# A twice-split channel MLP: p1 of two block pairs per group made of smaller products, their sums finished in their own PSUM tiles, in a new order

## The chip, the cores and the metric

The kernel runs on one core of a Trainium2 chip. The time is device microseconds of one execution; before the change the median of three runs is 792.29 us (792.07 to 792.38). The profiled execution is a further one. The core's engines are TensorE (PE; PEld is its weight load), VectorE (DVE), ScalarE (ACT), GpSimd (POOL) and SyncE (SP), each with a queue of its own that is worked off in order. Here SP issues nearly all transfers and POOL the rest.

## The reference

Hash attention over 4 batches, 8 heads, 768 positions of 64 features, then an MLP mixer over tokens and channels. The part that matters here is the last line, the channel MLP:

```python
xt = x.transpose(0, 2, 1)
h = np.maximum(xt @ w_tok1, 0.0) @ w_tok2
u = x + h.transpose(0, 2, 1)
h2 = np.maximum(u @ w_ch1, 0.0) @ w_ch2      # u: (4, 768, 512), w_ch1: 512x1536, w_ch2: 1536x512
return (u + h2).astype(np.float32)
```

All of it is in float32. A check on the attention's inputs (the `look`s) runs beside the channel MLP; a careful branch behind it is not taken with these inputs.

## The kernel before

The kernel has three stages: `attention` to about 310 us, `tokens` to 387 us, and `channels` to the end. The change lies in `channels`.

`channels` works on 3072 columns (4 batches of 768) in three groups s = 0, 1, 2 of 1024, a group being two slices of 512. Each group has a first layer (`hidden`, or `hidden_first` and `hidden_pair`), whose results go into four tiles R[0] to R[3], and a second layer (`outputs`, with `whole_product` and six calls of `product`). A matrix product is split in two by two blocks and computed with seven block products instead of eight (p1 to p7): the operands of p2 to p7 are blocks or sums of blocks, and the results are sums of the seven. `weight_sums` and `inputs` make such sums of the weights and of the columns.

In the first group the first layer's seven products are computed as they are (`hidden`, six times). In the groups s = 1 and 2 the rows come in three block pairs (t = 0, 1, 2, each of two blocks of 128 rows): `hidden_first` does t = 0 and `hidden_pair` t = 1 and 2. There p2, p3, p4, p6 and p7 (and p5 in `hidden_pair`) are split once more: each is a `Smaller`, seven products of 128 rows by 256 columns. `one` issues the first of them, `rest` three more into the same PSUM pair and `three` the last three into the pair where they are added to something else. Between these, `keep` (ScalarE) copies the first product out, `unite` (ScalarE) copies the sum of the first two, and `add` (VectorE, two instructions) makes the smaller results out of these in SBUF. p1, not a `Smaller`, is four products of 128 rows by 512 columns per block pair (`opened`); half of it is issued in the pair before (`open_next`). PSUM is four bank pairs, b0 to b3, taken in the order of `ring`; a `bank_pair` waits until all that used the pair before it has ended.

The right operands of a `Smaller` are made by `right_sums` (four VectorE instructions of 256 columns); its left operands, sums of the weights' quarters, are made once, in the preparation: `prepare` gives a list of jobs that the first group's `hidden` works off, one in the middle and one at the end of each call. A `parts` job makes four sums on VectorE (lines 1202 to 1205) in a tile of its own name, `seen`, or in a second area, and SP stores them to DRAM (`hidden_passed`, `passed`) with the quarters themselves (lines 1213 to 1223). Later `fetch_hidden_left` (line 871), `fetch_fifth` (879) and `fetch_left` (1273) bring them back on SP, each when the place has been read. `seen` has one buffer: a job that takes it waits until the store out of it has landed. The `look`s load into the same tile through POOL (line 1506) and work on it with two ScalarE activations (lines 1488 and 1496).

The order on each engine is the order of the program (a manual schedule). Two blocks in SBUF, `area(0)` and `area(1)`, hold the fetched left operands in front (`left_at`) and behind them output blocks: `output_at(0)` to `output_at(2)` in the one and `output_at(3)` in the other. In `hidden_first` p2's first product is copied into `output_at(2)` (`e2`, line 932 of `keep`). In `outputs` the results of the second layer's products take these blocks too, and `store` adds them to the output through POOL (line 1403).

## Time and profile before

The profiled execution took 793.06 us, its span from the first to the last instruction 791.3 us. The granted TensorE clock is 0.999.

| stretch | from, us | to, us |
|---|---|---|
| first group, first layer (with the preparation) | 387.2 | 459.1 |
| first group, second layer | 459.1 | 523.8 |
| second group, first layer | 523.8 | 591.15 |
| second group, second layer | 591.15 | 655.85 |
| third group, first layer | 655.85 | 721.75 |
| third group, second layer | 721.75 | 791.3 |

A line of the timeline has the start in the span, the length, the engine, the line of the kernel, what is written from what, its shape and how often; in square brackets the engine's idle time before it and what ended it. A TensorE record counts half a float32 product here, so "x6" is three products. Tile names are the program's: `second` is `area(0)` and `area(1)`, `TA` and `TB` hold the column sums, `SW` and `WC` the first layer's weights, `b` a PSUM pair. SPq and POOLq are the issue queues.

### The profile page before, as it was taken

The numbers are of one execution on the slowest core, as the hardware profiler recorded it, in microseconds if no ns is written. First come the engines' busy times: TensorE is split into PE (matmuls) and PEld (weight loads), VectorE is DVE, ScalarE is ACT, GpSimd is POOL, SyncE is SP. The second block draws the span as 40 slices with busy tenths as digits, with TensorE's granted clock in tenths as the row PEclk, the third lists the DMA queues.
The fourth block names the chain that finished last, engine by engine and source line by source line (L and its number), as shares of the span: only waits on it lengthen the run. The fifth ranks groups of instructions, "written<-read, shape, count | busy, mean of one in ns | idle before, by whom it ended". The sixth has DMA issues, their size and how long they took to land.

```text
span 791.3 us, 12505 instructions
## 1 busy us (share of the span) xinstructions
PE 784.1 (99%) x4721; PEld 476.3 (60%) x4721; DVE 656.8 (83%) x886; ACT 472.9 (60%) x817; POOL 53.7 (7%) x77
## 2 busy tenths in 40 slices
PE   9999999999999999999999999999999999999997
PEld 5444444444444444455544458877787887776886
DVE  5989898988987677999697798869879787978984
ACT  6688888888888886333323233536676674674331
POOL 1000000000000000011121010110001121000001
PEclk9999999999999999999999999999999999999999
DMA  4435353538352424795686995797847688830556
GB/s 164 163 123 163 123 164 123 163 124 248 144 175 87 142 60 164 210 265 119 119 267 230 343 367 182 228 303 200 274 128 231 242 243 213 252 92 0 184 161 140
DMA packets 102016, 144.85 MB, mean 183 GB/s; under 512 B 30200, under 2 KB 71616, under 8 KB 101952
## 3 DMA queue, kind: packets, MB, share of 16 engines
q1 hardware_dynamic: 93936, 119.15, 45.8%
q0 software_dynamic: 7728, 24.64, 14.0%
q8 instruction: 38, 0.62, 0.3%
q10 hardware_dynamic: 288, 0.21, 0.1%
q14 instruction: 26, 0.21, 0.1%
HBM read 101.01 MB, written 35.52 MB: 173 GB/s over the span
## 4 chain that ended last, share of the span: by engine, by line
PE 88%; issue 6%; DVE 2%; DMA 2%; POOL 1%; SPq 0%; ACT 0%; POOLq 0%; DVEq 0%; ACTq 0%
PE b L783 39%; PE sc L356 20%; PE acc L410 16%; PE t L656 5%; PE t L696 5%; PE sums L434 2%; PE hp L301 1%; DMA out<-second 1%; DMA hidden_left<-WC 0%; PE idle L473 0%; POOL out L1403 0%; PE hw L325 0%; POOL seen L1506 0%; DVE R L832 0%; DVE second L993 0%
## 5 line engine op out<-in xcount | busy, mean ns | idle before, releaser
L363 ACT ACTIVATE e<-sc 128x768 f32<-128x768 f32 x192 | 154.5, 810 | 6.4 <-PE sc L356 6.1
L356 PE MATMUL sc<-qk 64*128 64x384 f32 x768 | 152.6, 483 | 0.0
L783 PE MATMUL b<-R,second 128*128 128x256 f32 (+1 forms) x522 | 131.5, 409 | 0.0
L410 PE MATMUL acc<-e,vn 128*32 128x384 f32 x1536 | 127.0, 486 | 0.0
L783 PEld LDWEIGHTS b<-R,second 128*128 128x128 f32 x522 | 99.4, 190 | 29.1 <-issue 17.2
L395 DVE TENSOR_TENSOR esd<-esd,e 128x768 f32<-128x768 f32 x96 | 92.0, 958 | 10.4 <-ACT e L363 0.5
L410 PEld LDWEIGHTS acc<-e,vn 128*32 128x32 f32 x1536 | 50.1, 110 | 73.8 <-issue 73.4
L356 PEld LDWEIGHTS sc<-qk 64*128 64x128 f32 x768 | 68.2, 188 | 41.7 <-issue 37.2
L789 ACT COPY c<-b 128x256 f32<-128x256 f32 (+1 forms) x96 | 40.3, 426 | 80.6 <-PE b L783 70.4
L783 PE MATMUL b<-XT,WC 128*128 128x256 f32 (+1 forms) x228 | 74.0, 470 | 0.0
L356 PE MATMUL sc<-bits 64*128 64x384 bf16 x384 | 62.8, 324 | 0.1
L783 PEld LDWEIGHTS b<-XT,WC 128*128 128x128 f32 x228 | 43.3, 190 | 25.4 <-issue 20.0
L391 DVE SCALAR_TENSOR_TENSOR esd<-e 128x768 f32<-128x768 f32 x32 | 30.6, 956 | 23.4 <-ACT e L363 23.4
L783 PE MATMUL b<-XT,SW 128*128 128x256 f32 (+1 forms) x156 | 43.8, 413 | 0.4 <-DVE c L971 0.3
L656 PE MATMUL t<-x,W 128*128 128x512 f32 x96 | 41.8, 594 | 0.0
L356 PEld LDWEIGHTS <-bits 64*128 64x128 bf16 x384 | 18.6, 94 | 33.4 <-issue 9.7
L416 ACT ACTIVATE num<-acc,vsum 128x384 f32<-128x384 f32 x32 | 18.6, 581 | 29.8 <-PE acc L410 29.4
L783 PEld LDWEIGHTS b<-XT,SW 128*128 128x128 f32 x156 | 29.5, 190 | 11.0 <-issue 5.1
L716 POOL DMA_DIRECT2D XT<-second x8 | 9.8, 1228 | 383.1 <-DVE second L715 360.9
L455 ACT COPY rec<-rec 32x384 f32<-32x384 f32 x64 | 32.7, 510 | 5.0 <-DVE rec L449 4.2
L783 PE MATMUL b<-TA,WC 128*128 128x256 f32 (+1 forms) x92 | 33.7, 476 | 0.9 <-ACT c L932 0.9
L398 DVE TENSOR_TENSOR esd<-esd,e 128x768 f32<-128x768 f32 x32 | 30.5, 954 | 1.9
(245 smaller groups left out, 1219.3 us busy)
## 6 DMA issues: line engine op xcount, KB each, us to landing
second<-left SPq DMA_DIRECT2D x20, 768.0 KB
raw<-in_moe_w_ch SPq DMA_DIRECT2D x16, 768.0 KB
qk<-in_qk SPq DMA_DIRECT2D x15, 768.0 KB
second<-left SPq DMA_DIRECT2D x18, 576.0 KB
seen<-in_qk POOLq DMA_DIRECT2D x21, 384.0 KB, 4.8
WC<-hidden_left SPq DMA_DIRECT2D x18, 448.0 KB
vn<-in_v SPq DMA_DIRECT2D x16, 384.0 KB
vt<-in_vT SPq DMA_DIRECT2D x16, 384.0 KB
```

The source lines that it names most:

```text
L356: nc.tensor.matmul(sc[:, i, :HALF], t[rows, 1, P * c : P * c + P], t[rows, 0, qs], start=start, stop=not start,)
L363: nc.scalar.activation(e, sc[:, :, :HALF], ACT.Exp, scale=SCALE)
L391: nc.vector.scalar_tensor_tensor(self.d, es[0], NR * EPS, es[1], op0=ALU.add, op1=ALU.add,)
L395: nc.vector.tensor_tensor(self.d, self.d, e, op=ALU.add)
L398: nc.vector.tensor_tensor(self.d, self.d, self.es[-1], op=ALU.add)
L410: nc.tensor.matmul(acc[D * i + d : D * i + d + 32], vn[:, i, c, d : d + 32], e[:, i], start=(c == 0), stop=(c == NR - 1),)
L416: nc.scalar.activation(nums[self.n][:, self.half], acc, ACT.Identity, scale=-1.0, bias=vsum,)
L455: nc.scalar.copy(rec[other : other + 32, h], rec[at : at + 32, h])
L656: nc.tensor.matmul(ps, W1[:, r, P * j : P * j + P], x[:, r], start=(r == 0), stop=(r == NR - 1),)
L696: nc.tensor.matmul(ps[at], left, right, start=start, stop=True, skip_group_check=True,)
L783: nc.tensor.matmul(ps, left(k), right(k), start=start and k == ks[0], stop=stop and k == ks[-1], skip_group_check=True,)
L789: nc.scalar.copy(c, ps)
```

## The change

p1 of the block pairs t = 1 and 2 becomes a `Smaller` too. Its left operands need four more sums per row block: `first_parts` makes and stores them in the preparation, between p3's and p4's jobs, and `fetch_sums` (which was `fetch_fifth`) brings them for p1 as for p5. Its right operands are made in `hidden_first`, in the place of p3's; p3's are now made in the second layer of the group before.

`hidden_pair` has a new order. The sums of p1, p6 and p7 are finished in the PSUM tiles in which they were begun (`add(True)`, then `seed` copies three of the four back), and their last three products go into that same tile. The end of a pair is put off into the next one: p4's last three products, then the adds for r[1] and r[2] (`direct` and `end`), and the bounding of r[1] (`unbounded`). Each pair has one `look` instead of two, `hidden_first` two instead of three, and the first group's second layer two per product. In `hidden_first` p4's first product moves ahead of p3's `rest`.

In the second layer p2's block is `q5` (`output_at(3)`) instead of `q6` (`output_at(2)`). The fetch of the second left operand of a group's second layer moves from the second layer before it to the last block pair. The stores of p1's whole left operand and of the last p2 output are cut in more parts.

```diff
@@ end_rows
             if unfinished:
                 unfinished.pop()()
+            if unbounded:
+                unbounded.pop()()
@@ right_sums
             if name == "p5":
                 z = left_at(7 * s)[:, HC * 2 * P : HC * 2 * P + 2 * TT]
+            elif name == "p1":
+                z = left_at(7 * s + 1)[:, : 2 * TT]
@@ class Smaller
+            def seed(self):
+                nc.scalar.copy(self.ps[:, :3], self.e[:, :3])
@@
         def open_next(bank, s, t):
-            ahead.append(bank_pair(bank))
-            opened(ahead[0], [0], s, t + 1)
+            p1 = Smaller(None, "p1", s, t + 1)
+            p1.pair = bank_pair(bank)
+            p1.one(p1.pair, left_at(7 * s + 1)[:, 2 * TT : 4 * TT])
+            ahead.append(p1)
@@ hidden_first
             p4.three(V)
+            p4.one(bank_pair(x), e4)
             p3.rest()
...
-            p4.one(bank_pair(x), e4)
-            look()
@@ hidden_pair, the new order (the old one is in the listing)
+            A = p1.pair
+            if before:
+                before[0]()
+            B = bank_pair(two)
+            p6.one(B, e6)
+            if before:
+                before[1]()
+            p1.rest()
+            p1.unite()
+            C = bank_pair(three)
+            p2.one(C, e2)
+            p1.add(True)
             p6.rest()
+            p6.unite()
+            p1.seed()
+            p6.add(True)
             p2.rest()
             p2.unite()
+            p6.seed()
+            D = bank_pair(four)
+            p7.one(D, e7)
             p2.add()
+            p1.three(A)
+            if t + 1 == GP:
+                fetch_left(7 * s + 1)
+            copy_pair(first, A)
+            unbounded.pop()()
+            p6.three(B)
+            C = bank_pair(three)
+            p5.one(C, e5)
+            plus(u, flat(B), first)
+            p2.three(A)
+            look()
+            plus(r[0], banks(A), rows(e2))
             p5.rest()
+            p5.unite()
+            B = bank_pair(two)
+            p3.one(B, e3)
+            p5.add()
+            relu(r[0])
             p7.rest()
+            plus(flat(C), e5, u)
             p7.unite()
+            p7.add(True)
             p3.rest()
             p3.unite()
+            A = bank_pair(one)
+            p4.one(A, e4)
+            p7.seed()
+            p5.three(C)
             p3.add()
+            copy_pair(v, C)
             p4.rest()
             p4.finish()
+            p7.three(D)
+            plus(r[3], banks(D), rows(v))
             end_rows()
+            p3.three(C)
+
+            def direct():
+                p4.three(D)
+                plus(r[1], banks(C), rows(e3))
+
+            def end():
+                plus(e4, e4, u)
+                plus(r[2], banks(D), rows(e4))
+
+            later(r, (3, 2))
             if t + 1 < GP:
-                open_next(one, s, t)
+                open_next(two, s, t)
+                ring[:] = [two, three, one, four]
+                postponed.append((direct, end))
             else:
+                direct()
+                end()
@@ prepare
+            def first_parts():
+                def store(place, raw, rest):
+                    for i in range(0, 4, 2):
+                        nc.sync.dma_start(out=hidden_passed["p1"][:, i : i + 2], in_=place[:, i : i + 2])
+
+                return parts(first_weight("p1"), store)
...
-                [hidden_parts("p2"), fifth_parts], [hidden_parts("p6")], [hidden_parts("p3")], [hidden_parts("p4")],
+                [hidden_parts("p2"), fifth_parts], [hidden_parts("p6")], [hidden_parts("p3"), first_parts()],
+                [hidden_parts("p4")],
@@ product
-            looks = min(s + 1, 2) if s < last else 0
+            looks = 2 if s < last else 0
...
-            fetch_left(7 * s + j + 2, [0])
+            if j < 6:
+                fetch_left(7 * s + j + 2, [0])
@@ outputs
-            q3, q2, q4 = T[1], q6, q57
+            q3, q2, q4 = T[1], q5, q57
...
                 ], [
+                    right_sums("p3", s + 1)[0],
@@ at the end of channels
-            hidden_first(s, 0, [right_sums(name, s)[0] for name in ("p7", "p3", "p4", "p5")])
+            hidden_first(s, 0, [right_sums(name, s)[0] for name in ("p7", "p4", "p1", "p5")])
```

## The prediction

> **What bounds the kernel now.** I read the page first, for the engine that is never idle.
>
> ```profile
> PE 784.1 (99%) x4721; PEld 476.3 (60%) x4721; DVE 656.8 (83%) x886; ACT 472.9 (60%) x817; POOL 53.7 (7%) x77
> ```
>
> TensorE is busy nearly everywhere, so whatever stops it lengthens the span. VectorE is at 83%, and stage by stage closer: it runs without a gap where it is behind. Next come TensorE's own waits between 387 and 791 us (columns: total, times, longest), which is all it loses to other engines there:
>
> ```profile
> PE b L783 <- ACT c L932: 0.9, 1, 0.9
> PE b L783 <- DVE c L971: 0.3, 1, 0.3
> ```
>
> The chain of waits in order of time (start, length) says where these come from:
>
> ```profile
> 520.81 9.33 DMA out<-second
> ...
> 530.24 0.37 ACT second L932
> ...
> 542.19 0.44 DVE c L971
> ...
> 542.76 130.49 PE b L783 x546
> ```
>
> A store out of the block that p2's first sum goes into lands at 530.14; ScalarE, then VectorE, start late behind it, and TensorE meets VectorE's lateness until 542.76. Last, the timeline of three engines: TensorE in the first product of the second layer (start, length), VectorE, and the issues on SP.
>
> ```profile
> 470.72 1.46 PE L783 MATMUL b<-second 128*128 128x256 f32 x6
> 472.01 1.46 PE L783 MATMUL b<-c,second 128*128 128x256 f32 x6
> 473.31 6.64 PE L783 MATMUL b<-R,second 128*128 128x256 f32 x30
> ```
>
> ```profile
> 424.38 0.56 DVE L1202 TENSOR_TENSOR seen<-second 128x384 f32<-128x384 f32 x1 [2.28 <-DMA left<-seen]
> ...
> 461.55 0.55 DVE L1202 TENSOR_TENSOR seen<-WC 128x384 f32<-128x384 f32 x1
> ...
> 473.64 0.95 DVE L1348 TENSOR_TENSOR R<-R,c 128x768 f32<-128x768 f32 x1
> ...
> 531.56 0.96 DVE L993 TENSOR_TENSOR second<-b,second 128x768 f32<-128x768 f32 x1 [4.45 <-ACT second L996]
> ...
> 551.62 2.35 DVE L993 TENSOR_TENSOR R<-R,second 128x1024 f32<-128x1024 f32 x2
> ```
>
> ```profile
> 459.63 3.71 SPq L1223 DMA_DIRECT2D hidden_left<-SW  x4
> 463.78 0.32 SPq L1221 DMA_DIRECT2D hidden_left<-seen  x1
> ```
>
> See three things. Three products of 256 columns (six records) follow each other every 1.295 us: a unit, one 256-column product, is 0.432 us. The tile `seen` can't be rewritten before its store has landed (424.38 waited 2.28 us for that). And from 461.55 to 474.59 VectorE runs without a gap into L1348, whose result TensorE needs at 475.90 (473.31 plus two groups of 1.295).
>
> **TensorE's list.** A whole p1 block pair is four 512-column products, 8 units; in smaller ones it is 7. Four block pairs: 4 x 0.432 = 1.73 us less. From a group's first product (523.81 and 655.85) to its second layer (591.15 and 721.75) before takes 67.34 and 65.90 us for 151 units (65.2); after has 149 units, 64.3 us.
>
> **A new store in the preparation (price 5.8 us).** `first_parts` adds four VectorE sums (0.5 to 0.6 us each, as L1202 to L1205) and two stores of 384 KB between the preparation of p3 and that of p4. It takes `seen`, and p4's preparation takes `seen` again at once. Step by step: p3's sums go elsewhere and end at 459.15 as before. `seen` is free when the store issued at 453.88 has landed, by the trace's landing marks 459.66; first_parts' sums end at about 461.9. On SP its two stores stand behind p3's four (L1223, to 463.34). Between 442 and 469 us the DMA engines are busy throughout (share 1.02, 372 GB/s), so bytes land in the order queued: the two stores take the place that p4's 768 KB store has in before, issued 463.78, landed 468.52. So p4's sums start at about 468.55 instead of 461.55, 7.0 us late. Everything behind them in VectorE's queue shifts alike: L1348 ends at 481.6 instead of 474.6, with 0.15 us for the semaphore at 481.74, against 475.90. TensorE loses 5.8 us in three pieces (the two operands needed at 470.72 and 472.01 are late too). No idle TensorE time follows that could give it back. Bounds: the row at 421 us, nearly alone in the queue, has 3.3 us from issue to reuse, which from 463.43 gives 466.75 and 4.0 us; a landing 1 us later than taken gives 6.8. I take 5.8, as the queue is full there.
>
> [...]
>
> Behind this, p4's own stores and the fetch of p7's weights (L1273, 469.62) move to about 475; 1.3 MB at 372 GB/s is in by 480.5, needed at 478.5 + 5.8 = 484.3: covered by 3.8 us.
>
> **The place of p2's first sum (price in the next part).** p2's output moves to `q5`, the fourth block, so ScalarE need not wait 5.9 (first group) and 4.4 us (second). Then VectorE's `plus` at 531.56 starts when p2's three products end and the pair is copied: 523.81 + 12 units = 529.0, about 529.24. That is 2.3 us earlier in the first group, 1.1 in the second (662.15, where 655.85 + 5.43 = 661.3 would do). TensorE's waits of 0.94, 0.31 and (673.08) 0.28 go.
>
> **What is late next: VectorE at the first pair (price +1.4 us).** In before, VectorE works from 531.56 to 553.97 without a gap, 22.4 us up to the end of the first block pair's rows. After has the same list there (p1's four sums take the place of p3's; p3's move into the second layer's sixth product, where the operands behind them, from 509.96 on, have 3 us to spare). So the rows end at 529.24 + 22.4 = 551.65. Only then comes p1's `add` (0.72 + 0.42), and ScalarE's new `seed` of 768 columns (0.80, as L1111): 553.7 with the semaphores. TensorE's `p1.three` stands 64 units after 523.81, at 551.4, 551.75 with a short wait (0.2) for p7's sums at the moved `p4.one`. It waits 2.0 us; TensorE's whole queue waits behind it. Once past this, the pairs keep up: VectorE has 17.5 us in each (seven `add`s of 1.1, seven `plus` of 1.22, two bounded ones of 0.64) in 49 units, 21.2 us, and ScalarE, whose seeds are now three of 768 columns, gets 0.8 us more with one `look` of 2.0 us less. At the end of the last pair p4's three products come straight after p3's, without the p1 block between, and wait for `r[3]`: 0.2 + 1.23 + 0.15 behind p7's three, against 1.30, and a little for p4's `add`: 0.45. Sum: 64.3 + 0.2 + 2.0 + 0.45 and some 0.3 for taking up again = 67.3 us per group, against 67.34 and 65.90: 0.0 and +1.4. Bounds: all of it hidden is -1.73 - 0.94 - 0.31 - 0.28 = -3.3 us for both; VectorE 1 us later per group is +3.4.
>
> [...]
>
> **What costs nothing, and its cover.** Six more `look`s in the first group's second layer, one less in each block pair of the others: ScalarE is busy 26 of 65 us there, and the second group's layer (591 to 656) already has two per product with no TensorE wait; POOL, which issues their loads, waits for `seen` 5 us longer, with its next store due only at 502. The fetch of `left_at(7s+1)` moves on SP to the last pair's `p1.three`, some 25 us ahead of its use; behind it stand only next group's fetches. Two fetches of 256 KB per group (p1's sums) are wanted over 10 us after issue. `whole` p1's store in two, the last p2 output in four stores instead of three: one more issue of about 0.4 us each on SP, 8 us before the end. `r[3]`'s relu moves to the next pair or the layer's start, where the subtraction that needs it has over 2 us. Uncovered, each would cost its own length, under 1 us.
>
> **Sum.** +5.8 + 1.4 = +7.2 us. The profiled execution took 793.06 (span 791.3), 0.77 above the median of the three runs; against the median, 792.29 + 7.2 = **799.5 us**.
>
> **Rivals.** (1) The place is no wait, so that this part of the change does nothing: the stores land by 462.7 (461.55 plus the 1.16 us of slack before 475.90). Then +1.4 only: 793.7. For it: looks' DMAs on another queue show that landing order isn't strict; against: the full queue. (2) Faster: VectorE keeps ahead throughout, so that TensorE's list alone counts: 792.3 - 3.3 = 789.0. It decides only where VectorE's late queue at both places is made up, 7 us at the preparation and 2.0 at each first pair; for it speaks that ScalarE is freed by 4 to 6 us, against it that VectorE has no gap to close. (3) More is late: p7's weights, if the queue is 4 us slower than taken, stop TensorE once more for 2 to 3 us: 802.
>
> **How the numbers follow.** Forecast 0.66 (its own range 796.3 to 801.5, from 4.0 + 0 to 6.8 + 2.4), rival 1 0.13, rival 2 0.12, rival 3 0.09. The range takes in rival 1 and half of 3: 793.5 to 802. A difference of 0.2%, 1.6 us, is about what a measurement tells from none; rival 1, at 1.4, splits between same and slower: faster 0.12, same 0.06, slower 0.82.
>
> **What would show it.** Right: VectorE's first sum of p4's preparation waiting some 6 us for a store of `seen`; TensorE idle three times in the first product after the preparation, 5 to 6 us in all; ScalarE's copy of p2's first sum without a DMA wait; one TensorE wait of about 2 us for ScalarE's `seed` in each group's first pair and none of its size in the second; 7 units per p1. Wrong: TensorE without a gap at 470, or `seen` rewritten before its stores land, or a gap in every pair (then VectorE or the seeds bound the pairs, and the time is above the range).

## The result, and the profile after

The changed kernel takes 804.43 us (803.42 to 805.52) against 792.07 (791.31 to 792.38) for the kernel before on the same chip: a ratio of 1.0158 [1.0147, 1.0169], 12.4 us slower. The forecast was 799.5 with a range to 802.0: the direction was right, and the size was short by 4.9 us.

The profiled execution took 804.24 us (span 802.3) where that of before took 793.06 (span 791.3). So the two profiled executions are 11.2 us apart, and their traces place 11 of it as follows.

| stretch | before, us | forecast | after, us | measured |
|---|---|---|---|---|
| up to the first group's second layer | 459.12 | 0 | 459.34 | +0.2 |
| first group, second layer | 64.69 | +5.8 | 72.23 | +7.5 |
| second group, first layer | 67.34 | 0.0 | 68.97 | +1.6 |
| second group, second layer | 64.70 | 0 | 64.70 | 0.0 |
| third group, first layer | 65.90 | +1.4 | 67.29 | +1.4 |
| third group, second layer, to the end | 69.55 | 0 | 69.77 | +0.2 |

First again the page's busy times, now of the kernel after:

```profile
PE 788.1 (98%) x4745; PEld 483.0 (60%) x4745; DVE 665.5 (83%) x906; ACT 478.3 (60%) x825; POOL 53.8 (7%) x77
```

TensorE has less to multiply (149 units per first layer instead of 151, a unit being 0.432 us) and is busy for 4 us longer; busy time here is no measure of work, as a slower clock stretches it (below, six records take 2.77 us at a granted clock of 0.50, which took 1.46 at 1.00). VectorE's share is unchanged. What TensorE waits for between 387 and 802 us (line that waits, releaser: total, times, longest) has changed entirely:

```profile
PE b L783 <- ACT b L983: 4.0, 2, 2.0
PE b L783 <- DVE second L1334: 2.9, 1, 2.9
PE b L783 <- ACT c L789: 0.9, 2, 0.5
PE b L783 <- DVE R L1001: 0.4, 2, 0.2
```

Gone are the waits for `keep` (ScalarE) and `add` (VectorE) behind the late store of p2's block. New are two of 2.0 us for ScalarE's `seed` (L983), one of 2.9 behind the preparation, and 0.9 us for ScalarE's copies in the second layer. VectorE's timeline shows the place in the preparation (L1237 is the first sum of a job, L1391 was L1348):

```profile
461.21 0.56 DVE L1237 TENSOR_TENSOR seen<-WC 128x384 f32<-128x384 f32 x1 [1.76 <-DMA hidden_left<-seen]
...
469.89 0.56 DVE L1237 TENSOR_TENSOR seen<-WC 128x384 f32<-128x384 f32 x1 [4.07 <-DMA hidden_left<-seen]
...
481.83 0.95 DVE L1391 TENSOR_TENSOR R<-R,c 128x768 f32<-128x768 f32 x1
```

`first_parts` itself waits for the tile `seen` to be stored, and then p4's job waits for the two stores out of it. In before p4's job began at 461.55. TensorE (start, length) meets VectorE's lateness from 470.7 to 482.9:

```profile
464.49 6.61 PE L783 MATMUL b<-R,second 128*128 128x512 f32 x18
473.99 2.90 PE L783 MATMUL b<-second 128*128 128x256 f32 x6 [2.89 <-DVE second L1334]
476.68 2.77 PE L783 MATMUL b<-c,second 128*128 128x256 f32 x6
479.24 3.16 PE L783 MATMUL b<-R,second 128*128 128x256 f32 x12
482.92 1.32 PE L783 MATMUL b<-R,second 128*128 128x256 f32 x5 [0.52 <-ACT c L789]
```

The forecast had three idle pieces. There is one large one, and then six records take 2.77 us where before they took 1.46. The waits were swallowed by a TensorE at half speed. The view by stretches shows it (busy us and instructions of PE, PEld, DVE, ACT, POOL, then the granted clock, the DMA engines' share and GB/s), cut here at the borders where the clock changes:

```profile
469.81:473.22 3.41, 1.29 (x6) 0.78 (x5) 3.26 (x6) 1.39 (x2) 0.00 (x0) 1.00 0.10 41
473.23:476.64 3.41, 2.65 (x6) 2.19 (x7) 3.34 (x5) 0.00 (x0) 0.51 (x1) 0.50 1.01 384
476.64:480.06 3.42, 3.42 (x9) 2.70 (x8) 3.42 (x5) 1.29 (x4) 0.57 (x2) 0.50 1.01 331
480.06:483.47 3.41, 2.89 (x14) 2.24 (x13) 3.41 (x5) 0.93 (x3) 0.00 (x0) 1.00 1.02 408
558.56:561.97 3.41, 1.41 (x7) 0.93 (x6) 3.18 (x6) 1.24 (x3) 0.00 (x0) 1.00 1.06 408
561.97:565.38 3.41, 3.41 (x10) 2.69 (x9) 2.21 (x4) 2.01 (x3) 0.00 (x0) 0.50 0.64 238
691.68:695.10 3.42, 1.57 (x8) 1.04 (x6) 3.35 (x6) 0.96 (x2) 0.00 (x0) 1.00 1.01 364
695.10:698.51 3.41, 3.25 (x15) 2.90 (x16) 2.88 (x6) 2.56 (x5) 0.00 (x0) 1.00 0.16 53
```

The last four lines are the two waits of 2.00 us for `seed`, in the second group and in the third. Behind the first the clock is halved for 3.41 us; behind the second it is not. The rows of these waits:

```profile
561.59 0.88 PE L783 MATMUL b<-XT,WC 128*128 128x256 f32 x2 [2.00 <-ACT b L983]
562.26 1.06 PE L783 MATMUL b<-XT,SW 128*128 128x256 f32 x2
...
695.25 0.70 PE L783 MATMUL b<-XT,WC 128*128 128x256 f32 x2 [2.00 <-ACT b L983]
695.79 0.59 PE L783 MATMUL b<-XT,SW 128*128 128x256 f32 x2
```

The same wait and the same products: 68.97 us in one group and 67.29 in the other, so the halved clock is worth 1.7 us there.

### The profile page after: what moved, and what is told of

It reads as the page before. It is cut to its first block, busy times and chain, and to the rows that moved or that the text cites. A ratio compares the mean times of both kernels' runs of the same rounds, so it can differ in the third digit from the quotient of the medians.

```text
span 802.3 us, 12606 instructions
## 1 busy us (share of the span) xinstructions
PE 788.1 (98%) x4745; PEld 483.0 (60%) x4745; DVE 665.5 (83%) x906; ACT 478.3 (60%) x825; POOL 53.8 (7%) x77
## 4 chain that ended last, share of the span: by engine, by line
PE 83%; DVE 7%; issue 5%; DMA 3%; POOL 1%; ACT 0%; DVEq 0%; POOLq 0%; ACTq 0%
PE b L783 35%; PE sc L356 19%; PE acc L410 15%; PE t L656 5%; PE t L696 5%; DMA hidden_left<-seen 2%; PE sums L434 2%; DVE R L1001 1%; DMA looked<-in_qk 1%; PE hp L301 1%; DVE second L973 1%; DVE c L1001 1%; POOL seen L1551 0%; PE idle L473 0%; PE hw L325 0%
## 5 line engine op out<-in xcount | busy, mean ns | idle before, releaser
L395 DVE TENSOR_TENSOR esd<-esd,e 128x768 f32<-128x768 f32 x96 | 92.0, 958 | 10.4 <-ACT e L363 0.5
L783 PE MATMUL b<-XT,WC 128*128 128x256 f32 (+1 forms) x212 | 65.3, 445 | 4.0 <-ACT b L983 4.0
L783 PEld LDWEIGHTS b<-XT,WC 128*128 128x128 f32 x212 | 40.2, 190 | 24.5 <-issue 15.3
L783 PE MATMUL b<-XT,SW 128*128 128x256 f32 (+1 forms) x164 | 47.5, 413 | 0.0
L783 PEld LDWEIGHTS b<-XT,SW 128*128 128x128 f32 x164 | 31.4, 191 | 9.4 <-issue 4.1
```

The lines of the kernel that those rows point to most:

```text
L395: nc.vector.tensor_tensor(self.d, self.d, e, op=ALU.add)
L783: nc.tensor.matmul(ps, left(k), right(k), start=start and k == ks[0], stop=stop and k == ks[-1], skip_group_check=True,)
```

## The experiments

**p1's sums made where no tile is waited for.** The kernel after, with `first_parts` beside p6's second-layer job and in the place that `fifth_parts` has, so that it doesn't take `seen`:

```diff
             def first_parts():
-                def store(place, raw, rest):
-                    for i in range(0, 4, 2):
-                        nc.sync.dma_start(out=hidden_passed["p1"][:, i : i + 2], in_=place[:, i : i + 2])
+                quarter_parts("p1")
...
-                [hidden_parts("p7")], sums, [whole("p1"), second_parts("p7")], *([second_parts(name)] for name in ("p6", "p3", "p5", "p2", "p4")),
-                [hidden_parts("p2"), fifth_parts], [hidden_parts("p6")], [hidden_parts("p3"), first_parts()],
-                [hidden_parts("p4")],
+                [hidden_parts("p7")], sums, [whole("p1"), second_parts("p7")], [second_parts("p6"), first_parts],
+                *([second_parts(name)] for name in ("p3", "p5", "p2", "p4")),
+                [hidden_parts("p2"), fifth_parts], [hidden_parts("p6")], [hidden_parts("p3")], [hidden_parts("p4")],
```

> The changed kernel, with the sums for p1's left operands made earlier in the preparation (behind p6's second-layer parts) and in the place that p5's sums use, not in the shared tile. Theory (the shared tile's store holds VectorE): VectorE's wait of 4.1 us before p4's sums goes, the first group's second layer falls from 72.2 to about 65.2 us (64.7 as before, 0.5 for ScalarE's wait on the looks' loads), the clock stays full there; the two waits of 2.0 us in the first pairs stay. Time 804.4 - 7 = 797.4 us. Rival (the added transfers or the four added VectorE sums cost it, wherever they stand): at most half returns, the layer stays above 68 us and the time above 800.5.

797.4 us (796.92 to 798.05), ratio to before 1.0069 [1.0051, 1.0086]; 7.0 us less than the kernel after. The first second layer takes 64.88 us instead of 72.23. VectorE's same rows in this kernel:

```profile
461.38 0.55 DVE L1237 TENSOR_TENSOR seen<-WC 128x384 f32<-128x384 f32 x1
...
473.61 0.95 DVE L1390 TENSOR_TENSOR R<-R,c 128x768 f32<-128x768 f32 x1
```

Both are back to the times of before (461.55 and 473.64), although the four sums and their two stores are still made: it is the place that costs, not the work. The run changes two things together, the tile and the job's turn in the preparation; of the lateness in the kernel after, 1.76 and 4.07 us are waits for `seen`, the rest is the sums' own time. The two waits of 2.00 us are unchanged here, and the clock is again halved behind the first one only (first layers 68.96 and 67.28).

**The same job alone, in the kernel before.**

```diff
-                [hidden_parts("p2"), fifth_parts], [hidden_parts("p6")], [hidden_parts("p3")], [hidden_parts("p4")],
+                [hidden_parts("p2"), fifth_parts], [hidden_parts("p6")], [hidden_parts("p3"), first_parts()], [hidden_parts("p4")],
```

> The kernel before, with the new preparation job alone (four sums and two stores in the shared tile between p3's and p4's; nothing reads what it stores). Theory: the first group's second layer goes from 64.7 to 71.5 us, all else stays: 792.1 + 6.8 = 798.9 us. Blind sum: 792.1 + 5.8 = 797.9. Rival (the cost needs the rest of the change, the new looks or the fetches): under half of it, below 795.5 us.

799.77 us (799.54 to 801.46), ratio 1.0095 [1.0078, 1.0112]: +7.7 us, which is what the first second layer grows by in the trace (72.41 instead of 64.69); the other stretches are within 0.3 us of before, but for the last, which is 0.7 longer (this profile, 801.46, is of the longest of the four executions). TensorE there:

```profile
472.67 1.53 PE L783 MATMUL b<-second 128*128 128x256 f32 x6 [2.04 <-DVE second L1298]
474.65 1.53 PE L783 MATMUL b<-c,second 128*128 128x256 f32 x6 [0.45 <-DVE c L1301]
476.02 2.75 PE L783 MATMUL b<-R,second 128*128 128x256 f32 x12
481.60 5.81 PE L783 MATMUL b<-R,second 128*128 128x256 f32 x18 [2.83 <-DVE R L1355]
```

Here are the three pieces of the forecast, 5.3 us idle and 0.7 more from start to start of the products. p4's job began at 468.57, against 468.55 forecast. The rest of the 7.7 is in the last line: 18 records in 5.81 us. The stretches around it:

```profile
478.71:482.13 3.42, 0.59 (x4) 0.51 (x4) 3.42 (x5) 0.37 (x1) 0.00 (x0) 1.00 1.02 418
482.13:485.54 3.41, 3.41 (x10) 2.69 (x9) 3.34 (x6) 0.00 (x0) 0.00 (x0) 0.50 0.39 158
```

The halved clock falls behind the last wait, where nothing else is late: 1.7 us are lost. In the kernel after it falls between the waits, and VectorE hides it: the product at 482.92 waits for L1391, which ends at 482.78, and for ScalarE's copy of the slowed products, which ends at 482.81, so that the clock costs at most 0.03 us there.

**p1's right operands made earlier.** The kernel after, with p1's four right sums ahead of `hidden_first` instead of inside it:

```diff
-            hidden_first(s, 0, [right_sums(name, s)[0] for name in ("p7", "p4", "p1", "p5")])
+            right_sums("p1", s)[0]()
+            between = [right_sums(name, s)[0] for name in ("p7", "p4", "p5")]
+            hidden_first(s, 0, [*between[:2], lambda: None, between[2]])
```

> The changed kernel, with the four sums of p1's right operands made before the first block pair of a group instead of inside it. Theory (VectorE's list without a gap is what p1's last three products wait for, through the seed): 1.46 us go from that list, the waits of 2.00 us in both first pairs fall to about 0.5 us, the clock no longer halves in the second group; first layers 67.0 to 65.7 and 65.7 us from 69.0 and 67.3. Time 804.4 - 4.8 = 799.6 us, 801.3 where the clock had not halved. Rival (ScalarE's seed copies or their order are late by themselves): the waits stay at 1.7 to 2.0 us, time unchanged within 1 us.

803.38 us (801.38 to 806.12), ratio 1.0153 [1.0126, 1.018]: no gain that these times can show, and both waits for `seed` are still 2.00 us. (In the profiled execution, the shortest, the clock is not halved behind either: first layers 67.28 and 67.28.) My account of VectorE's list fell here. I had it run without a gap from p2's first sum on, so that whatever is taken out ahead would bring `seed` forward. Its rows in this kernel:

```profile
544.03 0.96 DVE L1001 TENSOR_TENSOR c<-b,c 128x768 f32<-128x768 f32 x1 [1.54 <-ACT c L1004]
...
548.69 0.69 DVE L973 TENSOR_TENSOR q<-b,second 128x512 f32<-128x512 f32 x1
...
556.51 2.35 DVE L1001 TENSOR_TENSOR R<-R,second 128x1024 f32<-128x1024 f32 x2
...
559.84 0.68 DVE L973 TENSOR_TENSOR q<-b,second 128x512 f32<-128x512 f32 x1
560.55 0.43 DVE L976 TENSOR_TENSOR b<-b,q 128x256 f32<-128x256 f32 x1
```

VectorE waits at 544.03 for a copy that itself waits for TensorE; the time gained is given back there. Its list is tied to TensorE again as late as p7's `add`: that starts at 548.69, and ScalarE's copy of p7's PSUM quarter, which it reads, ends at 548.65. From there on it has no such tie: 11.3 us up to p1's `add`, then 0.8 for ScalarE's `seed`, while TensorE has 24 units, 10.4 us, between the same two points. What shortens the wait must be taken out between these two.

**The idle TensorE filled.** The kernel after with four extra products ahead of `p1.three` in the pair t = 1, and six in the product of the first group that waits:

```diff
             p2.add()
+            if t == 1:
+                for _ in range(4):
+                    p7.mm(p7.ps[:, 3], 4, 0)
             p1.three(A)
...
+            if s == 0 and j == 1:
+                for _ in range(6):
+                    nc.tensor.matmul(
+                        B[:, 1, TT // 2 :], w[:, 0, 0], b00[:, 0], start=True, stop=True, skip_group_check=True,
+                    )
             part(b1, 1, extra(), True)
```

> The changed kernel with added products that nothing reads: four units ahead of p1's last three in each group's first pair, six units in the first wait of the first group's second layer, so that TensorE works where it waited. Theory (waits end when VectorE does; the halved clock after a wait costs 1.7 us in the second group, nothing in the first group's second layer, where VectorE is later still): no halved clock in the first pairs, the second group's first layer 69.0 to 67.3 us, the third's stays at 67.3, the first group's second layer stays within 0.3 of 72.2. Time 804.4 - 1.7 = 802.7 us. Rival (in that second layer the halved clock, not VectorE, sets the end): it falls by 3 us or more, time below 800.5.

813.02 us (811.63 to 817.99), ratio 1.0257 [1.0233, 1.0281]. It failed as a test of the clock, as the fill did not fill. TensorE and ScalarE in the second group's pair:

```profile
566.06 3.05 PE L783 MATMUL b<-TA,WC 128*128 128x256 f32 x8 [3.47 <-ACT q L937]
```

```profile
563.73 0.80 ACT L983 COPY b<-second 128x768 f32<-128x768 f32 x1 [2.46 <-DVE b L976]
...
565.64 0.37 ACT L937 COPY q<-b 128x256 f32<-128x256 f32 x1
```

The PSUM quarter that the extra products write is read by `keep`, which stands on ScalarE behind the very `seed`s that are late; the wait grew from 2.00 to 3.47 us, and now the clock was halved in both groups. In the first group's product the extra work only moved the idle to the third wait (2.82 us), with the halved clock behind it. What it does give is rows for the clock (below).

**The two adds between taken out.** VectorE's last two adds of `hidden_first` (the 2.35 us at 556.51 above) moved behind p2's `add` of the next pair, in the kernel after:

```diff
             p4.finish()
-            plus(r[1], r[1], rows(e3))
-            plus(r[2], r[2], rows(e4))
+
+            def last():
+                plus(r[1], r[1], rows(e3))
+                plus(r[2], r[2], rows(e4))
+
+            lasts.append(last)
...
             p2.add()
+            if lasts:
+                lasts.pop()()
             p1.three(A)
```

> The kernel after, with VectorE's last two additions of each group's first block pair (the bounded sums r1 and r2, 2.35 us together) moved behind p2's addition of the second pair, so that p1's addition and ScalarE's three-block copy into p1's PSUM tile (the seed) come 2.35 us earlier. Theory (TensorE's 2.0 us wait at p1's second products, once in each group, is VectorE's gapless list from the point where ScalarE's copy of p7's first quarter releases it; the halved TensorE clock behind that wait is a consequence of it): the wait of 2.0 us goes to under 0.3 in both groups, no halved clock follows there, both first layers take 65.3 us, and the time is 804.4 - 2 x 2.0 - 1.7 (the halved clock in the second group) = 798.7 us, or 800.4 against a run of the kernel after without the halved clock there. Rival (what is late is ScalarE's own list, not VectorE's): the wait stays between 1.5 and 2.0 and the time between 803 and 804.5. Second rival (the two additions are only late next, in front of p2's second products): the wait moves to them, first layers of 66.5 to 67.3, 801 to 804.

799.73 us (797.43 to 800.11), ratio 1.0083 [1.0062, 1.0105]: 4.7 us less than the kernel after. Both waits for `seed` are gone, no clock is halved there, and both first layers take 65.50 us (68.97 and 67.29). TensorE in the place:

```profile
558.99 0.59 PE L783 MATMUL b<-TA,WC 128*128 128x256 f32 x2
559.42 0.59 PE L783 MATMUL b<-XT,WC 128*128 128x256 f32 x2
...
565.40 0.70 PE L783 MATMUL b<-XT,SW 128*128 128x256 f32 x2 [0.21 <-DVE c L1001]
```

The two first layers give back 5.3 us in the trace, where 4.0 of idle and 1.7 of halved clock were expected; a new wait of 0.21 us comes 6 us later. The whole execution gives back less: its first second layer took 72.59 (here the halved clock behind the preparation's last wait, from 482.45 on, has nothing later to hide behind), and the second group's second layer 65.54 instead of 64.70, with two waits of 0.16 us.

**p2's block alone.** First in the kernel before, the block as the only edit:

```diff
-            q3, q2, q4 = T[1], q6, q57
+            q3, q2, q4 = T[1], q5, q57
```

> The kernel before with one part of the change alone: p2's output of the second layer's sixth product goes into the fourth block instead of the second. Theory (the wait of ScalarE's and VectorE's copies for the store out of that block is what makes TensorE wait 0.94, 0.31 and, in the second group, 0.28 us): these three waits go, the first layers take 66.1 and 65.6 us instead of 67.34 and 65.90, and the time is 792.05 - 1.5 = 790.5 us. Rival (VectorE's next list takes their place, or another store is late in the fourth block): 791.5 to 792.5, no difference that can be measured.

791.27 us (790.79 to 791.95), ratio 0.9983 [0.9975, 0.9992]. The trace is clear: TensorE has no wait left in either group, the first layers take 65.55 and 65.54 us (67.34 and 65.90), and the span is 789.0 us. ScalarE's copy of p2's first sum, which in before came at 530.24 behind the store:

```profile
527.74 0.37 ACT L932 COPY second<-b 128x256 f32<-128x256 f32 x1 [3.49 <-PE b L783]
```

Then the reverse: the kernel after with p2's output back in the second block (the same line, turned round).

> The kernel after with p2's output of the sixth product back in the second block. Theory (VectorE's list in the first pair starts afresh where ScalarE's copy of p7's first quarter releases it, so a late start of p2's first sum is partly made up before that point): ScalarE's copy of p2's first sum waits for the store again, TensorE waits about 1.3 us in the second group's first layer as before did, and p1's wait stays at 2.0: 804.4 + 0.3 to 1.5, 804.7 to 805.9 us. Rival (the list is one without gaps from p2's first sum on, so that a later start makes p1's wait longer by the same): p1's waits are 4.3 and 3.1 us, and the time is 807.5 or more.

804.77 us (802.22 to 807.26), ratio 1.0165 [1.0144, 1.0187], which the times can't tell from the kernel after. ScalarE waits for the store again:

```profile
535.40 0.37 ACT L937 COPY second<-b 128x256 f32<-128x256 f32 x1 [4.12 <-DMA out<-second]
```

In the first layers TensorE waits 2.00 us for `seed`, twice, as with the new block, and once 0.35 us for VectorE. The expected 1.3 us was not there: the copy comes 4.7 us after the layer's start (530.71), in before 6.4. The rival, that p1's wait would grow to 4.3 and 3.1, is refuted. But the theory's reason holds in part only. p2's sum starts 6.01 us after the layer's start (5.43 in the kernel after), p7's `add` 18.25 us after it (17.83), and TensorE waits for the result:

```profile
548.96 0.68 DVE L973 TENSOR_TENSOR q<-b,second 128x512 f32<-128x512 f32 x1
550.25 0.67 PE L783 MATMUL b<-TB,SW 128*128 128x256 f32 x2 [0.35 <-DVE q L976]
```

Of the 0.58 us of lateness 0.42 is still there at p7's `add`. Then TensorE is held back with VectorE, and p1's wait behind it stays 2.00. The late p2 is thus paid for at that place: this first layer is 67.70 us, the third group's, without the wait, 67.29.

**The kernel before, profiled again.** This asks why the profiled executions are 11.2 us apart and the medians 12.4.

> The kernel before once more, for a second profile of it: the profiled execution that the prediction was made from took 793.06 us, 0.8 to 1.0 above the median. Theory (that execution's excess is the store out of the second block that landed at 530.14 in the second group, with TensorE's waits of 0.94 and 0.31 behind it; it mostly lands earlier): an execution of 791.7 to 792.3 us has a first layer of 65.9 to 66.3 us there, as in the third group (65.90), instead of 67.34, and no wait over 0.5. Rival (the waits are there each time, and the excess is spread or lies ahead of the layers): 67.0 to 67.4 again, with the waits of 0.9 and 0.3.

The second profiled execution took 793.27 us (span 791.4), with the waits of 0.93 and 0.30 us in the same places, and first layers of 67.43 and 65.73. So the waits are not an accident of one execution. But the theory spoke of an execution of 791.7 to 792.3 us, and this one was again of 793: whether a shorter one has the waits is not shown. The other seven executions of this run lie between 790.6 and 792.06, median of all eight 791.5. The kernel before it was compared with, the same program, had 792.54 in 21 executions, from 790.76 to 793.75, six of them above 793.1; the ratio is 0.9986 [0.9976, 0.9996]. Three things follow. Both profiles of this kernel are of executions from the upper end of its own spread; what makes one long or short stays open. The same program can differ from itself by 0.14%, so that the 0.9983 of the block alone, and anything like it, is not told from no change by the times. And a difference of spans compares two single executions: that of the block alone is 2.3 us from a long execution of before, while the medians differ by 1.0 (792.31 and 791.27).

**Both causes taken away.** The kernel after with the first and the fifth edit of this section together:

> The kernel after with both causes taken away: p1's sums of the weights made beside p6's second-layer parts, in the place that p5's have, so that the tile that p4's preparation waits for isn't taken, and VectorE's last two additions of each group's first block pair moved behind p2's addition of the second pair. Theory: the first second layer takes 64.9 us (0.2 above before), both first layers 65.3 (before 67.34 and 65.90), the rest as in the kernel after: 0.2 + 0.2 - 2.0 - 0.6 + 0.2 = -2.0, 790.1 us, faster than both kernels. Rival (the waits taken away turn into others, or p1's sums in their new place delay the preparation): 792.5 or more.

791.73 us (791.12 to 793.0), ratio 0.9994 [0.9984, 1.0003]. In the trace the waits are gone as the theory has it, with a span of 789.4 against 791.3 of before (-1.9; -2.0 expected, but against that long execution), second layer 64.79, first layers 65.50 and 65.50. By the times it is no faster than before: the 790.1 us of the theory are not reached. And it is no better than the block alone, although TensorE has two units (0.86 us) less in each first layer. Where these went, in the waits of TensorE:

```profile
PE b L783 <- DVE c L1001: 0.4, 2, 0.2
PE b L783 <- DVE R L1001: 0.4, 2, 0.2
```

One wait of 0.2 us of each kind in each group. From start to start of the products each costs 0.45 us and a little more: the eight records from 556.36 on, four units or 1.73 us, take until 558.56 around an idle time of 0.21, 0.47 us longer. Twice 0.45 eats the 0.86.

**One of these waits attacked.** In the last kernel, the two bounded subtractions (1.29 us of VectorE) of each pair moved from ahead of the sum `u` to behind it:

```diff
             copy_pair(first, A)
-            unbounded.pop()()
             p6.three(B)
...
             plus(u, flat(B), first)
+            unbounded.pop()()
             p2.three(A)
```

> The kernel with both causes taken away (p1's sums made beside p6's second-layer parts; the first pair's last two additions behind p2's addition of the second), and in each pair VectorE's two bounded subtractions (1.29 us) moved from ahead of the sum u to behind it. In the trace of the kernel without this move TensorE loses 0.47 us in each group at 557.44, where p3's first product waits for that sum (0.21 idle, the rest of it in starting again), and 0.45 at the end of the last pair, where p4's products wait for r3. Theory (VectorE's list is still 0.2 us late there and has room behind it): the wait for u goes, the first layers take 65.0 us instead of 65.5, and the time is 791.7 - 2 x 0.47 = 790.8 us; the wait for r3 stays. Rival (the room behind it is not there): another wait of 0.2 to 0.4 us takes its place within 10 us, and the time stays at 791.5 to 792.

792.15 us (791.23 to 793.16), ratio 0.9998 [0.9989, 1.0007]. The rival: the wait for `u` is gone and one of 0.21 us takes its place 3.5 us further into the layer (562.68, for the sum that p5 is started from). VectorE has no room there. In this profile TensorE also waits 0.79 us at the end of the first group's second layer:

```profile
PE b L783 <- ACT c L789: 0.8, 1, 0.8
PE b L783 <- DVE b L1001: 0.4, 2, 0.2
```

**The looks put back.** The first line above is ScalarE held up behind a `look` whose load was 10.5 us on its way. In the kernel after its chain of waits (start, length) goes through such a load, and TensorE is 0.39 us late behind it, at 529.78:

```profile
518.91 10.08 DMA looked<-in_qk
...
530.17 18.80 PE b L783 x70
```

So, in the kernel with both causes taken away, the looks as before had them:

```diff
-            looks = 2 if s < last else 0
+            looks = min(s + 1, 2) if s < last else 0
...
             p4.finish()
+            look()
             p7.three(D)
...
             p3.finish()
+            look()
             nc.scalar.copy(r[2][:, 1, 1], rows(u)[:, 1, 1])
```

> The kernel with both causes taken away (p1's sums made beside p6's second-layer parts; the first pair's last two additions behind p2's addition of the second), and with the looks where the kernel before has them: one in each product of the first group's second layer, two in each pair and three in the first. Theory (the second look in each product stops ScalarE's queue for its load in some executions, 1.13 us and 1.53 us in two profiles, and then TensorE for 0.39 and 0.79 behind it; in the others it costs nothing): no such wait at the end of the first group's second layer, 64.7 us for it, no new wait in the pairs, and 791.7 - 0.2 to 0.4 = 791.3 to 791.5 us. Rival (ScalarE has no room for the looks in the pairs any more, now that it copies three blocks at each seed): waits for ScalarE of 0.5 to 1 us in the pairs, 792.5 us or more.

793.11 us (792.6 to 793.55), ratio 1.0008 [0.9999, 1.0017], 1.4 us above the kernel without this edit (on another chip, where before was 0.2 us higher too); the spans differ by 1.7. The second layer takes 64.69 us without a wait, as expected; the profile of the kernel without this edit had none there either (64.79), so it isn't shown that the place of the looks took it away. And a worse one has come:

```profile
PE b L783 <- ACT second L937: 1.3, 2, 0.7
PE b L783 <- DVE c L1001: 0.4, 2, 0.2
```

```profile
545.43 0.85 ACT L1540 ACTIVATE looked<-looked 128x768 f32<-128x768 f32 x1
546.31 0.94 ACT L1548 ACTIVATE looked<-looked,minus_safe 128x768 f32<-128x768 f32 x1
...
547.54 0.36 ACT L937 COPY second<-b 128x256 f32<-128x256 f32 x1
```

A third `look` in `hidden_first` is 2 us of ScalarE just ahead of a `keep` that TensorE waits for, 0.65 us in each group (0.91 from start to start). So in the new order the looks are not free at their old place, and at their new one they cost TensorE 0.39 and 0.79 us in two profiles.

**The clock over all these traces.** Where a profile shows several halved stretches, their borders lie on one grid of 3.413 us: in the kernel after 561.97 - 473.23 = 88.74 = 26 x 3.413, in the filled one 566.84 - 481.51 = 85.33 = 25 x 3.413 and 703.37 - 481.51 = 221.86 = 65 x 3.413. The other five of the table have one halved stretch each, of 3.41 us, and the grid is counted from its border. Counted back, the first border lies between 0.2 and 3.2 us into the span, in each profile at another point. TensorE's busy time in a stretch of that grid, from the view by stretches, and the clock in the next one:

| kernel | stretch from, us | TensorE busy of 3.41 | clock next |
|---|---|---|---|
| job alone | 478.71 | 0.59 | 0.5 |
| filled | 699.96 | 0.58 | 0.5 |
| two adds moved | 479.04 | 0.65 | 0.5 |
| filled | 563.43 | 0.78 | 0.5 |
| old block | 470.68 | 1.24 | 0.5 |
| after | 469.81 | 1.29 | 0.5 |
| filled | 478.09 | 1.29 | 0.5 |
| operands earlier | 470.83 | 1.38 | 0.5 |
| after | 558.56 | 1.41 | 0.5 |
| p1's sums elsewhere | 550.67 | 1.41 | 0.5 |
| operands earlier | 689.29 | 1.54 | 1.0 |
| after | 691.68 | 1.57 | 1.0 |
| old block | 559.43 | 1.71 | 1.0 |
| two adds moved | 468.80 | 1.94 | 1.0 |
| operands earlier | 559.58 | 2.12 | 1.0 |

In all fifteen rows the next stretch was halved behind at most 1.41 us busy, and not behind at least 1.54. The halved stretches in which TensorE was busy nearly throughout (3.35 us and more) were followed by a full one; behind those with 2.65 (after, 473.23), 2.72 and 2.78 us busy (filled, 481.51 and 703.37) the clock stayed at 0.5 for a second one. So where a wait of 2.00 us fell in the grid went with whether it cost 1.7 us more: whole in one stretch (after, 558.56) it did, cut in two (old block, 559.43) it did not. That the grid and the busy share are the cause was read from these traces, not tried by moving one wait along the grid.

The executions without a profile, for which the time and the mean granted clock are on record, agree with that price. With p1's operands made earlier they are 802.36 us at 0.997, 804.39 at 0.994 and 806.12 at 0.992; with the two adds moved, 797.43 at 0.999 and 799.79 at 0.997. A mean clock that is lower by 0.005 is 8 us of halved clock in 800, 4 us of work lost. In the kernel after itself, where part of it is hidden, the order is not so clean (803.42 us at 0.994, 803.88 at 0.997).

## Why the prediction was right or wrong

**A new store in the preparation (price 5.8 us): right in its mechanism, 1.7 us short.** The tile `seen`, the four sums, the two stores, p4's job behind them and TensorE idle in the first product are as described, and the two edits of this place alone show it from both sides (-7.0 and +7.7 us). Three terms were off in the kernel after. p4's job began at 469.89, not 468.55: counted from the start of the second layer (459.34, not 459.12), 1.1 us later. The step that failed is "the two stores take the place that p4's 768 KB store has in before, issued 463.78, landed 468.52": already the store issued at 454.11 landed at 461.19 (7.1 us; 5.8 in before), and the two of `first_parts`, issued from 462.89 on, landed at 469.8. In the kernel with the job alone they landed as forecast, and in the other four profiles with these stores in this place p4's job began, counted in the same way, 0.1 to 0.4 us later than forecast, so this execution was the late one. Its DMA engines, as busy as in before (a share of 0.99 in both), moved 295 GB/s between 442 and 452 us, where before has 334; why is not settled. The second term is the 0.39 us of idle at 529.78 (0.65 from start to start), which "what costs nothing" had at zero: "six more `look`s" are not free when their loads take 10 us. 5.8 + 1.1 + 0.65 = 7.55, measured 7.54. The third is the clock, next. (The three idle pieces of the forecast are in the kernel with the job alone; in the kernel after there are one of 2.89 us, slowed products, and one of 0.52.)

**What the sum left out: the halved clock.** No step priced what a wait of 2 us does to the products behind it. In the second group this is +1.7 us and all of that row's miss (0.0 forecast, +1.6 measured). In the preparation of the kernel after it is hidden; in the kernel with the job alone it is 1.7 of the 7.7. The channel MLP in the trace of before could not have shown it: its longest wait there is 0.94 us, and the clock falls only at 789.97, behind TensorE's last product.

**What is late next: size and engines right, the start of the list wrong.** The wait of 2.0 us at `p1.three` in each group's first pair, none in the second pair, ScalarE's `seed` as its releaser, a small wait at the last pair's end, and +1.4 us in the third group are all as forecast. In the kernel after the count itself comes out: VectorE works from p2's first sum, 5.43 us into the layer, to the end of the pair's rows in 22.6 us (22.4 forecast), and `p1.three` starts 30.0 us into the layer (29.9 forecast). But the step "the rows end at 529.24 + 22.4 = 551.65" takes the start at p2's sum for what sets the end, and that did not hold. Copies of TensorE's results hold the list on its way too, p7's `add` last of all. With 1.46 us taken out ahead of that, the wait stayed 2.00; with p2's sum 0.58 us later, it stayed 2.00 as well; with 2.35 us taken out behind it, it was gone. The 2.0 us is, to 0.15 us, the difference between 11.3 + 0.8 us of work on VectorE and ScalarE and 10.4 of TensorE from there, with 0.14 us on the way from the one engine to the next (in the kernel after, 560.65 to 560.73 and 561.53 to 561.59). That both counts give 2.0 was luck; the first would send an engineer to the wrong part of the list, as it sent me in the run with p1's operands earlier.

**The place of p2's first sum: right.** The copy no longer waits for a store, the waits of 0.94, 0.31 and 0.28 are gone. It was put too low if anything: alone it is 2.3 us of span and 1.0 of the medians, where these three are 1.5; the first layers gain 1.79 and 0.36 us, since a wait costs more than its idle time (in before, 541.00 to 543.27 is 2.27 us for four units, 0.54 too long with 0.31 of idle). (Two readings in that step were off, without weight in the sum: from 662.15 to 661.3 is 0.9 us, not 1.1, and the 0.28 at 673.08 is a gap between two products that the list of waits doesn't have.)

**TensorE's list: right.** 149 units instead of 151. The bound "all of it hidden" assumed that waits can be had at zero; the best order tried here still pays 0.9 us per group for two short ones.

**The base.** The sum stood against the median, while the profiled execution was 0.8 above it, one of the long ones of this kernel. The profiled executions differ by 11.2 us, the medians by 12.4. Of the miss of 4.9 us, 4.0 is in the terms above (1.7 in the place, 1.6 in the clock, the rest in small shifts at both ends), 1.2 in this difference, and -0.2 in the median of before, which is now 792.07. The range left out most of this: the upper end that it was counted up to, 801.5, had the place at 6.8 and 2.4 for VectorE, though the bound for VectorE 1 us later per group is 3.4 by its own words (802.5 in all), and neither the clock nor the base.

**The rivals.** Rival 1 (the place is no wait) and rival 2 (VectorE keeps ahead) are refuted by the trace. Rival 3 came nearest in size, "more is late", but with the wrong culprit: p7's weights stopped nothing.

## What to carry to other kernels

A job added to a filled preparation cost here by the tile that it borrowed, not by its instructions: the same four sums and two stores cost 7 us in a tile that the next job waits for, and 0.2 in another and earlier in the preparation. To price VectorE's lateness, find the last instruction in its list that needs a fresh result of the bound engine, and count from there; 1.46 us of work taken out ahead of that point bought nothing, and 2.35 us moved from behind it removed a wait of 2.0. And a TensorE wait can have a second price: 1.7 us for the stretch of halved clock behind the wait of 2.00 us in the second group, at most 0.03 behind the one of 2.89 in the preparation of the kernel after, where VectorE was later still, and none behind the same 2.00 in the third group, where the clock stayed full.

## What the runs showed of the hardware that was not expected

- The granted TensorE clock fell to 0.50 for one or two stretches of 3.41 us behind stretches of the grid in which TensorE was busy for 0.58 to 1.41 us (ten rows of the table), and stayed at 1.00 behind those with 1.54 to 2.12 (five rows); it came back behind halved stretches that were busy for 3.35 us and more. An idle time of 2.00 us was enough in the kernel after, where it lay whole in one stretch (558.56 to 561.97).
- A wait of 0.21 us cost 0.47 us from start to start of the products (both causes taken away, 556.36 to 558.56), one of 2.00 cost 2.27 (after, 692.66 to 695.79, where two units take 0.86).
- The same 768 KB out of one tile landed 4.74 us after its issue as one store (before, 463.78 to 468.52); as two of 384 KB it landed 6.9 us after the first issue in the kernel after (462.89 to 469.8). p4's job, which waits for the two, began at 469.89 there and between 468.57 and 469.30 in four other profiles with the same stores (job alone, two adds moved, operands earlier, old block).
